# Attention ahead of a mixture of experts: where the softmax's reciprocals stand, and when its sums and scalings are issued

## The chip, the cores and the metric

The kernel runs on one core of one Trainium2 chip. The time is that of one execution on the device in microseconds; several executions give a median. Lower is better.

## The reference

Three stages follow each other; the change lies in the first, and the other two only wait for its result.

```
q_pool = q.reshape(B, H, S // 2, 2, D).mean(axis=3)      # B 4, H 8, S 1152, D 64: 576 pooled queries
scores = matmul(q_pool, k^T) / sqrt(D)                   # 576 x 1152 for each of 32 heads
attn   = exp(scores - max(scores))
attn   = attn / (sum(attn) + 1e-9)
x      = matmul(attn, v)                                 # 576 x 64 a head, together x[2304, 512]
x      = moe(x, w_gate, w1, w2)                          # 8 experts, Sinkhorn gate
out    = soft_moe(x, phi, m2_w1, m2_w2)
```

## The kernel before, in words

A phase is one head; two heads form a pair, so there are 16 pairs and 32 phases (NPH). A phase has nine slots (SLOTS), one for each 128 keys, and the main loop of `attention` goes through all slots `s` in one row: `ph` is the phase, `c` the slot in it, `u` the slot in the pair (0 to 17). What an engine does, and in which order, is written out by this loop: PE, ScalarE, VectorE and GpSimd execute what the loop emits in that order.

In each slot, `emit_E` computes the transposed scores of 128 keys against the 576 queries into one of two PSUM tiles `se` (L255), ScalarE takes the exponential into a tile `e` (L260), and GpSimd adds `e` to the running sum `acc` of the phase (L264, L266). Both inputs of that addition and its output lie in SBUF. The maxima that the exponential needs are computed a phase ahead: `emit_S` writes scores the other way round into one of two PSUM banks `S` (L226), and VectorE reduces them (L227). `first(n)` emits the next n of these, so that L226 waits for the L227 two steps before it. `emit_nm` (L230) and `emit_row` (L239, L243, L245) turn the maxima into a row that is added in the products of `emit_E`.

At the slots u = 0, 5, 9 and 14 (RUNS) there is a run: all products of `e` with v that are due (`emit_PV`, L281, into the bank `o`) are issued in one row, with two S steps ahead of them and two behind. u = 0 and 9 have c == 0, u = 5 and 14 have c == 5. A run at c == 0 finishes the phase before, and ScalarE copies `o` to the SBUF tile `oc` (L288).

The normalisation of phase ph - 1 begins at c == 5 of phase ph: `emit_sum` multiplies `acc` by ones (L296), which gives the sum over the keys on all partitions, and ScalarE writes it with 1e-9 added to the SBUF tile `rs` (L300). At c == 0 of phase ph + 1 `emit_recip` takes the reciprocals in place, in two halves of 144 columns (L304). At c == 5 of that phase `emit_O` multiplies: four operations, for each of two groups of 64 partitions one with 256 columns into the tile of x (L313) and one with 32 into the ninth tile (L314). Of the 288 columns the first 256 and the last 32 go to different tiles, `xa[2 * b + g]` and `xa[8]`.

`bank()` gives the one PSUM bank `t` (pool `ps_t`, one buffer). It is shared by the transposes of k and q (`k_bank`, `q_bank`, L163, L134), by `emit_row` and by `emit_sum`; a new user waits for the last reader of the one before. Behind the transposes of k these are ScalarE's copy (L170) and VectorE's subtraction L176, which reads `t` from PSUM and `kp` from SBUF; behind those of q, L150 and L152. The subtractions are put off by `low` and issued by `flush` behind the `emit_E` of the next slot. k's second bank is filled at u = 13, so its L176 comes just ahead of the run at u = 14; q's first one is filled at u = 3 and its L152 comes ahead of the run at u = 5.

In the last phase VectorE adds a part of the running sums itself (L272), and the loop goes on for ten slots behind it: at c == 0 phase 30 is normalised, at c == 3 the last sums are formed, at c == 6 phase 31 is normalised. From there on the matmuls of the first expert (L777 to L779 and, behind them, L796) run, with VectorE and ScalarE splitting weights and activations into high and low parts.

Of the kernel before, what the change touches and what calls it, by code (L numbers as in the profile page):

```python
# [11 lines left out]
ALU = mybir.AluOpType  # L12
# [14 lines left out]
def attention(ctx, nc, tc, q, k, v, xa, ident, ones, hooks):  # L27
# [18 lines left out]
    NPH = 2 * NPAIR  # L46
    raws = {n: {} for n in "qkv"}
    prep, M_, E_, acc_, O_, R_ = {}, {}, {}, {}, {}, {}
# [51 lines left out]
    def bank():  # L100
        return ps_t.tile([128, 512], F32, tag="t", name="t")
# [7 lines left out]
    def flush():  # L109
        while later:  # L110
            later.pop(0)()
# [66 lines left out]
    def k0(pi):  # L178
        k_bank(pi, 0, 4, half() if front[0] else bank())

    def k4(pi):
        k_bank(pi, 4, 4, half() if front[0] else bank())

    def kq8(pi):
        ps = bank()
        k_bank(pi, 8, 1, ps)
        o, st = qd[pi % 2], prep[pi]
        src = ps[:, 128:256].rearrange("p (h g x) -> p h g x", h=2, g=2)
        q1 = st["q1"][:, :, :, 256:]
        for h in range(2):  # L190
            nc.scalar.copy(o[64 * h:64 * h + 64, 64 * h:64 * h + 64], ps[64 * h:64 * h + 64, 128 + 64 * h:192 + 64 * h])
        nc.scalar.copy(q1, src)
        low(lambda: nc.vector.tensor_tensor(
            out=q1[64:128], in0=src[64:128], in1=q1[64:128].bitcast(F32), op=ALU.subtract
        ))
# [33 lines left out]
    def emit_nm(ph, x0, n):  # L229
        nc.vector.tensor_reduce(  # L230
            out=NM[ph % 2][:, x0:x0 + n, 64], in_=M_[ph][:, x0:x0 + n], axis=AX.X, op=ALU.max, negate=True
        )

    def emit_row(ph, x0, n):
        pi, h = divmod(ph, 2)
        q2 = prep[pi]["q2"][64:65]
        ps = bank()
        for x in range(n):
            nc.tensor.matmul(  # L239
                ps[:65, 128 * x:128 * x + 128], lhsT=NM[ph % 2][:, x0 + x], rhs=identr, start=True, stop=True  # L240
            )
        if x0 == 0:
            nc.scalar.copy(q2[:, :, :, 256:], ps[64:65, :128].rearrange("p (h g x) -> p h g x", h=2, g=2))  # L243
        else:
            nc.scalar.copy(q2[:, h, :, :256], ps[64:65].rearrange("p (g x) -> p g x", g=2))  # L245


    def emit_E(ph, c, between=0):
        pi, h = divmod(ph, 2)
        st, kd = prep[pi], KD[ph % 3]  # L250
        e = E_[ph, c] = e_p.tile([128, 2, 288], F32, tag="e", name="e")
        ps = ps_e.tile([128, 2, 512], F32, tag="se", name="se")[:, :, :288]
        for g in range(2):
            for z, y in enumerate((st["q1"], st["q2"])):
                nc.tensor.matmul(  # L255
                    ps[:, g], lhsT=kd[:, z, 128 * c:128 * c + 128], rhs=y[:, h, g], start=z == 0, stop=z == 1
                )
            if g == 0:
                first(between)
        nc.scalar.activation(out=e, in_=ps, func=AF.Exp, scale=1.0 / 16)  # L260

        if c == 1:
            acc_[ph] = sm_p.tile([128, 2, 288], F32, tag="acc", name="acc")
            nc.gpsimd.tensor_tensor(out=acc_[ph], in0=E_[ph, 0], in1=e, op=ALU.add)  # L264
        elif c > 1 and (ph < NPH - 1 or c < LATE):
            nc.gpsimd.tensor_tensor(out=acc_[ph], in0=acc_[ph], in1=e, op=ALU.add)  # L266
        elif c == 8:
            acc_["end"] = e
        elif c > LATE:
            if c == LATE + 1:  # L270
                acc_["late"] = sm_p.tile([128, 2, 288], F32, tag="acc", name="acc")
            nc.vector.tensor_tensor(  # L272
                out=acc_["late"], in0=E_[ph, LATE] if c == LATE + 1 else acc_["late"], in1=e, op=ALU.add
            )

    def emit_PV(ph, c):
        pi, h = divmod(ph, 2)
        if c == 0:
            O_[ph] = ps_o.tile([128, 512], F32, tag="o", name="o")
        for g in range(2):  # L280
            nc.tensor.matmul(  # L281
                O_[ph][64 * g:64 * g + 64, :288], lhsT=raws["v"][pi][:, h, c, :], rhs=E_[ph, c][:, g],
                start=c == 0, stop=c == 8,
            )
        E_.pop((ph, c))
        if c == 8 and ph < NPH - 1:
            o = sm_p.tile([128, 288], F32, tag="oc", name="oc")
            nc.scalar.copy(o, O_[ph][:, :288])  # L288
            O_[ph] = o

    def emit_sum(ph):
        ps = bank()
        ts = [acc_.pop(ph)] + ([acc_.pop("end"), acc_.pop("late")] if ph == NPH - 1 else [])
        for j, t in enumerate(ts):
            for g in range(2):
                nc.tensor.matmul(  # L296
                    ps[64 * g:64 * g + 64, :288], lhsT=ones[:, :64], rhs=t[:, g], start=j == 0, stop=t is ts[-1]
                )
        R_[ph] = sm_p.tile([128, 288], F32, tag="rs", name="rs")
        nc.scalar.activation(out=R_[ph], in_=ps[:, :288], func=AF.Identity, bias=eps)  # L300

    def emit_recip(ph, u):
        r = R_[ph][:, 144 * u:144 * u + 144]
        nc.vector.reciprocal(out=r, in_=r)  # L304

    def emit_O(ph):
        pi, h = divmod(ph, 2)
        b, hp = pairs[pi]
        o, r = O_.pop(ph), R_.pop(ph)
        for g in range(2):  # L310
            y, z = slice(64 * g, 64 * g + 64), slice(64 * h, 64 * h + 64)
            w = slice(64 * b + 32 * g, 64 * b + 32 * g + 32)
            nc.vector.tensor_tensor(out=xa[2 * b + g][z, hp, :], in0=o[y, :256], in1=r[y, :256], op=ALU.mult)  # L313
            nc.vector.tensor_tensor(out=xa[8][z, hp, w], in0=o[y, 256:288], in1=r[y, 256:], op=ALU.mult)  # L314

    firsts = [(2 * p + (x > 4), x if x < 5 else x - 4, n) for p in range(NPAIR) for x in range(9) for n in range(3)]

    def first(n=1):
        for _ in range(n):
            if firsts:  # L320
                emit_S(*firsts.pop(0))
# [31 lines left out]
    for s in range(SLOTS * NPH + 10):  # L353
        ph, c = divmod(s, SLOTS)
        pi, h = divmod(ph, 2)
        u = s % (2 * SLOTS)
        nxt, nn = pi + 1, pi + 2
        on, run = ph < NPH, u in RUNS if ph < NPH else s % 3 == 0
        for f in hooks.get(s - SLOTS * NPH, ()):
            with tc.issue_after(last_dma[0]):  # L360
                f()
        if on:
            emit_E(ph, c, int(u in BETWEEN or s in (2, 4)))
            flush()
        if run:
            if on:
                first(2)
            if 1 < ph <= NPH and c == 0:
                emit_recip(ph - 2, 0)
                emit_recip(ph - 2, 1)  # L370
            if ph > 1 and (c == 5 if on else c == 0):
                emit_O(ph - 2)
            if ph == NPH and c == 6:
                emit_recip(ph - 1, 0)
                emit_recip(ph - 1, 1)
            for g in range(max([x for x in range(s) if x % (2 * SLOTS) in RUNS], default=0), s):
                if g < SLOTS * NPH:
                    emit_PV(*divmod(g, SLOTS))
            if ph and (c == 5 if on else ph == NPH and c == 3):
                emit_sum(ph - 1)  # L380
            if on:
                first(2)
        if ph + 1 < NPH and u in (5, 14):
            emit_nm(ph + 1, 1, 4)
        if ph + 2 < NPH and u == 8:
            emit_nm(ph + 2, 0, 1)
        if ph + 1 < NPH and u in (6, 15):
            emit_row(ph + 1, 1, 4)
        if ph + 1 < NPH and u == 10:
            emit_row(ph + 1, 0, 1)  # L390
        if on and nxt < NPAIR:
            if s == 0:
                k0(nxt)
            if s == 2:
                k4(nxt)
            if u == (3 if s < SLOTS else 1):
                kq8(nxt)
            if u == (4 if s < SLOTS else 2):
                kd_dma(nxt, 0)
            if u == (4 if s < SLOTS else 3):  # L400
                q_bank(nxt, 0)
            if u == 8:
                q_bank(nxt, 1)
            if u == 9:
                q2_dma(nxt)
                kd_dma(nxt, 1)
                load_v(nxt)
        if on and nn < NPAIR:
            if u == 6:
                load_k(nn)  # L410
                load_q(nn)
            if u in (11, 13):
                pool_q(nn, u // 13)
            if u == 12:
                k0(nn)
            if u == 13:
                k4(nn)
# [1061 lines left out]
```

## Time and profile before

| | |
|---|---|
| Median of three executions | 2242.56 us (2242.03 to 2244.97) |
| The profiled execution, its own time | 2243.12 us |
| Its span in the profile | 2241.2 us |
| Attention stage | about the first 640 us of the span |
| Granted TensorE clock, mean over the span | 0.987 of full |
| Busy: PE, VectorE, ScalarE, GpSimd | 2099.8, 1497.4, 944.1, 412.6 us |

The span runs from the first to the last instruction; the execution's own time is 1.9 us longer. Busy time counts an engine's instructions from start to end; matmuls overlap in the pipeline and their ends are modelled, so PE reads as busier than it is. In a timeline the second column is a duration, `xN` means that N neighbouring records were merged, and what stands in brackets at the end is how long the engine had been idle and which instruction ended that.

### The profile page before, as it was taken

The page shows a single profiled execution, that of the slowest core. Times are in us where ns is not written, and L with a number is a line of the kernel's source. Part 1 is how long each engine was busy: PE and PEld are TensorE (multiplying, and loading weights), DVE is VectorE, ACT ScalarE, POOL GpSimd, SP SyncE. Part 2 cuts the span into 40 slices and gives each one's busy share as a digit, 9 for nine tenths or more (in the row PEclk, how much of TensorE's full clock was granted, in tenths as well). Part 3 has the DMA queues.
Part 4 walks back from the last instruction along what each step waited for, and adds up shares of the span by engine and source line. Part 5 has one row for each costly group of instructions (what it writes and reads, how often), then busy time and mean ns, then how long its engine had stood idle before and what let it go on. Part 6 is the DMA issues. An engine that isn't in the chain of part 4 may idle for free.

```text
span 2241.2 us, 40342 instructions
## 1 busy us (share of the span) xinstructions
PE 2099.8 (94%) x16382; PEld 1904.5 (85%) x16382; DVE 1497.4 (67%) x2529; ACT 944.1 (42%) x1708; POOL 412.6 (18%) x304
## 2 busy tenths in 40 slices
PE   7888888788899999999999999999999999999997
PEld 5665656565689999999999999999999999999864
DVE  5777777777785867668667757757766855544462
ACT  3444444444454445345336435435534533311232
POOL 5666666666610000000000000000000000000000
PEclk9999999999999999999999999999999999999998
DMA  7443435343332555454456445536445523487569
GB/s 176 111 96 96 111 80 119 88 106 69 86 113 114 214 191 169 168 192 159 151 198 207 160 160 184 208 127 209 168 167 178 177 74 123 151 327 264 207 218 281
DMA packets 175273, 358.41 MB, mean 160 GB/s; under 512 B 49392, under 2 KB 98096, under 8 KB 173104
## 3 DMA queue, kind: packets, MB, share of 16 engines
q1 hardware_dynamic: 172688, 354.35, 49.8%
q8 instruction: 130, 2.13, 0.4%
q10 hardware_dynamic: 2400, 1.47, 0.2%
q14 instruction: 55, 0.45, 0.1%
HBM read 274.81 MB, written 48.23 MB: 144 GB/s over the span
## 4 chain that ended last, share of the span: by engine, by line
PE 76%; DVE 16%; ACT 5%; issue 2%; DMA 1%; SPq 1%; ACTq 0%; DVEq 0%
PE y L796 28%; PE g L738 15%; PE seed L738 9%; DVE m L227 4%; PE se L255 4%; DVE x L313 3%; DVE rs L304 2%; PE S L226 2%; ACT e L260 2%; DVE x L314 2%; PE g L828 1%; PE g L829 1%; PE g L827 1%; PE y L848 1%; PE g L777 1%
## 5 line engine op out<-in xcount | busy, mean ns | idle before, releaser
L796 PE MATMUL y<-v,ho 128*128 128x256 f32 x5292 | 679.8, 284 | 3.7 <-DVE acc L808 2.6
L796 PEld LDWEIGHTS y<-v,ho 128*128 128x128 f32 x5292 | 653.8, 192 | 9.8 <-issue 4.4
L738 PE MATMUL g<-xs,w 128*128 128x256 f32 x2880 | 375.9, 283 | 0.0
L738 PEld LDWEIGHTS g<-xs,w 128*128 128x128 f32 x2880 | 359.0, 192 | 0.0
L266 POOL TENSOR_TENSOR acc<-acc,e 128x576 f32<-128x576 f32 x218 | 310.5, 1424 | 94.9 <-ACT e L260 82.7
L227 DVE TENSOR_REDUCE m<-S 128x1 f32<-128x384 f32 x432 | 226.1, 550 | 90.3 <-PE S L226 83.3
L952 POOL MEMSET HT<- 128x1024 f32 x2 | 1.9, 960 | 1484.9 <-PE g L829 1484.9
L808 DVE SCALAR_TENSOR_TENSOR acc<-y,P,acc 128x256 f32<-128x256 f32 x378 | 181.4, 480 | 117.3 <-PE y L796 114.5
L260 ACT ACTIVATE e<-se 128x576 f32<-128x576 f32 x288 | 183.7, 653 | 167.0 <-PE se L255 131.0
L712 DVE TENSOR_TENSOR ho<-hr,ho 128x512 fp32r<-128x512 f32 x189 | 130.2, 689 | 150.3 <-ACT ho L711 148.3
L738 PE MATMUL seed<-xs,w 128*128 128x256 f32 x1728 | 211.3, 283 | 0.0
L738 PEld LDWEIGHTS seed<-xs,w 128*128 128x128 f32 x1728 | 209.1, 192 | 0.0
L712 DVE TENSOR_TENSOR ho<-ht,ho 128x512 fp32r<-128x512 f32 x252 | 170.3, 686 | 50.7 <-ACT ho L711 48.5
L711 ACT CAST ho<-ht 128x512 fp32r<-128x512 f32 x252 | 150.3, 618 | 112.4 <-DVE ht L705 110.2
L255 PE MATMUL se<-q,kd 128*128 128x288 f32 x576 | 187.4, 333 | 5.6 <-ACT e L260 4.6
L226 PE MATMUL S<-kd,q 128*128 128x384 f32 x384 | 126.0, 377 | 60.0 <-DVE m L227 59.5
L255 PE MATMUL se<-qm,kd 128*128 128x288 f32 x576 | 172.5, 307 | 0.0
L281 PE MATMUL o<-e,vr 128*64 128x288 f32 x1152 | 154.4, 413 | 0.0
L226 PEld LDWEIGHTS S<-kd,q 128*128 128x128 f32 x384 | 67.9, 196 | 93.0 <-DVE m L227 56.7
L255 PEld LDWEIGHTS se<-q,kd 128*128 128x128 f32 x576 | 114.4, 199 | 17.9 <-ACT e L260 16.5
L281 PEld LDWEIGHTS o<-e,vr 128*64 128x64 f32 x1152 | 77.3, 137 | 60.9 <-issue 16.8
L705 DVE TENSOR_TENSOR ht<-hr 128x512 f32<-128x512 f32 x126 | 86.2, 684 | 54.1 <-ACT hr L747 31.8
(210 smaller groups left out, 3080.8 us busy)
## 6 DMA issues: line engine op xcount, KB each, us to landing
stg<-in_moe_w_dram SPq DMA_DIRECT2D x96, 512.0 KB, 6.0
kd<-kp SPq DMA_DIRECT2D x31, 576.0 KB, 5.7
xs<-xd0B SPq DMA_DIRECT2D x34, 512.0 KB, 4.1
xs<-xd1B SPq DMA_DIRECT2D x34, 512.0 KB, 4.1
xs<-xd2B SPq DMA_DIRECT2D x34, 512.0 KB, 4.0
xs<-xd3B SPq DMA_DIRECT2D x34, 512.0 KB, 4.3
fd<-stg SPq DMA_DIRECT2D x24, 512.0 KB, 5.7
stg<-fd SPq DMA_DIRECT2D x24, 512.0 KB, 4.5
```

What stands on the lines that cost most here:

```text
L226: nc.tensor.matmul(ps, lhsT=w, rhs=r[:, 384 * n:384 * n + 384], start=True, stop=True)
L227: nc.vector.tensor_reduce(out=M_[ph][:, x, n:n + 1], in_=ps, axis=AX.X, op=ALU.max)
L255: nc.tensor.matmul(ps[:, g], lhsT=kd[:, z, 128 * c:128 * c + 128], rhs=y[:, h, g], start=z == 0, stop=z == 1)
L260: nc.scalar.activation(out=e, in_=ps, func=AF.Exp, scale=1.0 / 16)
L266: nc.gpsimd.tensor_tensor(out=acc_[ph], in0=acc_[ph], in1=e, op=ALU.add)
L281: nc.tensor.matmul(O_[ph][64 * g:64 * g + 64, :288], lhsT=raws["v"][pi][:, h, c, :], rhs=E_[ph, c][:, g], start=c == 0, stop=c == 8,)
L705: (eng or nc.vector).tensor_tensor(out=o, in0=a, in1=b, op=op)
L711: nc.scalar.copy(o[:, 0], p)
L712: nc.vector.tensor_tensor(out=o[:, 1], in0=p, in1=o[:, 0].bitcast(F32), op=ALU.subtract)
L738: nc.tensor.matmul(o, lhsT=w[:, a, kk, cols], rhs=x[:, b, kk], start=begin, stop=kk == 1 and z == 2, skip_group_check=not first or f2 > 0,)
L796: nc.tensor.matmul(ps, lhsT=o[:, x, c], rhs=v[:, w, c], start=first and c + z == 0, stop=c + z == 5, skip_group_check=not first,)
L808: nc.vector.scalar_tensor_tensor(out=y, in0=ps, scalar=p, in1=y, op0=ALU.mult, op1=ALU.add)
```

## The change

The reciprocals no longer replace the sums in SBUF. Each half of 144 columns is written to a fresh `bank()` in PSUM, and the multiplications of that half follow at once and read it from there. The first half's part is issued at c == 0, the second half's at c == 5, both for phase ph - 2 as before. The second half has 112 columns for the tile of x and 32 for the ninth tile, so a phase now has two reciprocals and six multiplications where it had two and four. In the last phase the reciprocals stay in place. `emit_sum` is issued ahead of the products with v of its run, and ahead of the reciprocal, where it used to come behind the products.

```
--- before.py
+++ after.py
@@ -299,19 +299,21 @@
         R_[ph] = sm_p.tile([128, 288], F32, tag="rs", name="rs")
         nc.scalar.activation(out=R_[ph], in_=ps[:, :288], func=AF.Identity, bias=eps)
 
-    def emit_recip(ph, u):
-        r = R_[ph][:, 144 * u:144 * u + 144]
-        nc.vector.reciprocal(out=r, in_=r)
-
-    def emit_O(ph):
+    def emit_O(ph, u):
         pi, h = divmod(ph, 2)
         b, hp = pairs[pi]
-        o, r = O_.pop(ph), R_.pop(ph)
+        o, r, n = O_[ph], R_[ph][:, 144 * u:144 * u + 144], 144 * u
+        t = bank()[:, :144] if ph < NPH - 1 else r
+        nc.vector.reciprocal(out=t, in_=r)
         for g in range(2):
             y, z = slice(64 * g, 64 * g + 64), slice(64 * h, 64 * h + 64)
             w = slice(64 * b + 32 * g, 64 * b + 32 * g + 32)
-            nc.vector.tensor_tensor(out=xa[2 * b + g][z, hp, :], in0=o[y, :256], in1=r[y, :256], op=ALU.mult)
-            nc.vector.tensor_tensor(out=xa[8][z, hp, w], in0=o[y, 256:288], in1=r[y, 256:], op=ALU.mult)
+            m = min(n + 144, 256)
+            nc.vector.tensor_tensor(
+                out=xa[2 * b + g][z, hp, n:m], in0=o[y, n:m], in1=t[y, :m - n], op=ALU.mult
+            )
+            if u:
+                nc.vector.tensor_tensor(out=xa[8][z, hp, w], in0=o[y, 256:288], in1=t[y, 112:144], op=ALU.mult)
 
     firsts = [(2 * p + (x > 4), x if x < 5 else x - 4, n) for p in range(NPAIR) for x in range(9) for n in range(3)]
 
@@ -365,19 +367,22 @@
         if run:
             if on:
                 first(2)
-            if 1 < ph <= NPH and c == 0:
-                emit_recip(ph - 2, 0)
-                emit_recip(ph - 2, 1)
-            if ph > 1 and (c == 5 if on else c == 0):
-                emit_O(ph - 2)
-            if ph == NPH and c == 6:
-                emit_recip(ph - 1, 0)
-                emit_recip(ph - 1, 1)
+            if ph and (c == 5 if on else ph == NPH and c == 3):
+                emit_sum(ph - 1)
+            if ph > 1 and on:
+                if c == 0:
+                    emit_O(ph - 2, 0)
+                else:
+                    emit_O(ph - 2, 1)
+            elif ph == NPH and c == 0:
+                for j in range(2):
+                    emit_O(ph - 2, j)
+            elif ph == NPH and c == 6:
+                for j in range(2):
+                    emit_O(ph - 1, j)
             for g in range(max([x for x in range(s) if x % (2 * SLOTS) in RUNS], default=0), s):
                 if g < SLOTS * NPH:
                     emit_PV(*divmod(g, SLOTS))
-            if ph and (c == 5 if on else ph == NPH and c == 3):
-                emit_sum(ph - 1)
             if on:
                 first(2)
         if ph + 1 < NPH and u in (5, 14):
```

VectorE, in the first head of the second pair, from the run at c == 0 to the run at c == 5 (`m` are the maxima, `nm` their negative, `oc` the copy of the products with v, `x_80`, `x_81` and `x_88` the tiles of x). At c == 0:

```order
 L230 TENSOR_REDUCE nm_121<-m_405 128x4
 L227 TENSOR_REDUCE m_596<-S 128x1 x4
-L304 RECIPROCAL rs<-rs 128x144 x2
+L307 RECIPROCAL t<-rs 128x144
+L312 TENSOR_TENSOR x_80<-oc,t 64x144
+L312 TENSOR_TENSOR x_81<-oc,t 64x144
 L227 TENSOR_REDUCE m_596<-S 128x1 x3
```

One reciprocal has given way to two multiplications of 144 columns. At the next c == 5, on VectorE:

```order
 L152 TENSOR_TENSOR q_540<-t,q_540 64x2x256
 L227 TENSOR_REDUCE m_596<-S 128x1 x2
-L313 TENSOR_TENSOR x_80<-oc,rs 64x256
-L314 TENSOR_TENSOR x_88<-oc,rs 64x32
-L313 TENSOR_TENSOR x_81<-oc,rs 64x256
-L314 TENSOR_TENSOR x_88<-oc,rs 64x32
-L227 TENSOR_REDUCE m_762<-S 128x1 x2
+L307 RECIPROCAL t<-rs 128x144
+L312 TENSOR_TENSOR x_80<-oc,t 64x112
+L316 TENSOR_TENSOR x_88<-oc,t 64x32
+L312 TENSOR_TENSOR x_81<-oc,t 64x112
+L316 TENSOR_TENSOR x_88<-oc,t 64x32
+L227 TENSOR_REDUCE m_766<-S 128x1 x2
```

The second reciprocal stands here now, ahead of four multiplications with 112 and 32 columns in place of 256 and 32; the maxima behind them are the same (their tile has another number). On PE, at the run at c == 5 in the second head of the first pair (`S` scores for the maxima, `t` the bank, `o` the products with v):

```order
 L226 MATMUL S<-kd_125,q_303 128x384 x2
+L296 MATMUL t<-acc,ones 64x288 x2
 L281 MATMUL o<-e,vr 64x288 x10
-L296 MATMUL t<-acc,ones 64x288 x2
 L226 MATMUL S<-kd_123,q_303 128x384 x2
```

The two sums have moved ahead of the ten products with v; the pairs of S on either side stay. At the end of the stage 35 matmuls of the first expert now stand between the last products with v and the last sums, where the sums used to follow directly; ScalarE, GpSimd and the queue of SyncE have the same order as before.

## Rows read from the trace of the kernel before

**Rows 1.** Busy time of each engine in one stretch of the attention stage.

```profile
430.00:580.00 150.00, 120.95 (x796) 88.41 (x793) 113.16 (x187) 66.51 (x128) 98.41 (x70) 0.98 0.40 94
```

**Rows 2.** Chain of waits from 195 to 260 us, its shares by line.

```profile
by line: DVE m L227 16.2%; PE se L255 13.9%; DVE x L313 12.0%; DVE rs L304 11.8%; ACT e L260 8.0%; PE S L226 7.5%; DVE x L314 6.6%; DVE kp L176 4.7%; issue 4.6%; PE t L163 3.3%; DVE q L152 3.2%; ACT q L150 2.4%; ACT kp L170 1.8%; ACT qm L24
```

**Rows 3.** Groups of VectorE's instructions by form, 0 to 640 us: count, busy, mean ns.

```profile
L313 DVE TENSOR_TENSOR x<-oc,rs 64x256 f32<-64x256 f32 x62 | 69.7, 1124 | 1.4
L304 DVE RECIPROCAL rs<-rs 128x144 f32<-128x144 f32 x64 | 62.7, 1022 | 0.4
L314 DVE TENSOR_TENSOR x<-oc,rs 64x32 f32<-64x32 f32 x62 | 50.1, 808 | 0.0
...
L176 DVE TENSOR_TENSOR kp<-t,kp 128x512 fp32r<-128x512 f32 x32 | 22.0, 687 | 21.9 <-ACT kp L170 21.8
...
L176 DVE TENSOR_TENSOR kp<-t,kp 128x128 fp32r<-128x128 f32 x16 | 4.7, 291 | 17.1 <-PE S L226 16.8 <-ACT kp L170 0.3
...
L313 DVE TENSOR_TENSOR x<-o,rs 64x256 f32<-64x256 f32 x1 | 0.4, 419 | 0.1
...
L314 DVE TENSOR_TENSOR x<-o,rs 64x32 f32<-64x32 f32 x1 | 0.2, 174 | 0.0
```

**Rows 4.** Timeline, a run at c == 5 in a second head: start, duration, instruction.

```profile
242.67 0.69 DVE L176 TENSOR_TENSOR kp<-t,kp 128x512 fp32r<-128x512 f32 x1
...
243.51 0.63 PE L163 MATMUL t<-ident,kr 128*128 128x128 f32 x4 [1.17 <-DVE kp L176]
...
244.79 0.69 DVE L176 TENSOR_TENSOR kp<-t,kp 128x512 fp32r<-128x512 f32 x1 [1.43 <-ACT kp L170]
...
244.94 2.65 PE L281 MATMUL o<-e,vr 128*64 128x288 f32 x20
...
246.45 1.25 DVE L313 TENSOR_TENSOR x<-oc,rs 64x256 f32<-64x256 f32 x1
...
247.38 1.59 POOL L120 TENSOR_TENSOR qp<-qr 128x576 f32<-128x576 f32 x1
247.42 0.66 PE L296 MATMUL t<-acc,ones 128*64 128x288 f32 x4
247.62 1.40 DVE L314 TENSOR_TENSOR x<-oc,rs 64x32 f32<-64x32 f32 x1
...
248.00 0.62 PE L226 MATMUL S<-kd,q 128*128 128x384 f32 x2
248.12 0.50 ACT L300 ACTIVATE rs<-t,eps 128x288 f32<-128x288 f32 x1 [2.70 <-PE t L296]
...
248.93 1.39 POOL L266 TENSOR_TENSOR acc<-acc,e 128x576 f32<-128x576 f32 x1
...
249.03 1.58 DVE L313 TENSOR_TENSOR x<-oc,rs 64x256 f32<-64x256 f32 x1
...
250.75 1.02 DVE L227 TENSOR_REDUCE m<-S 128x1 f32<-128x384 f32 x2
...
251.36 0.44 PE L226 MATMUL S<-kd,q 128*128 128x384 f32 x1 [2.48 <-DVE m L227]
```

**Rows 5.** Timeline, a run at c == 5 in a first head.

```profile
224.47 0.69 DVE L152 TENSOR_TENSOR q<-t,q 64x512 fp32r<-64x512 f32 x1 [0.84 <-ACT q L150]
...
225.16 2.65 PE L281 MATMUL o<-e,vr 128*64 128x288 f32 x20
...
228.22 0.63 PE L226 MATMUL S<-kp,qd 128*128 128x384 f32 x2
...
229.66 1.01 DVE L227 TENSOR_REDUCE m<-S 128x1 f32<-128x384 f32 x2
```

**Rows 6.** Timeline, a run at c == 0.

```profile
235.94 1.97 DVE L304 RECIPROCAL rs<-rs 128x144 f32<-128x144 f32 x2
...
237.82 0.50 DVE L227 TENSOR_REDUCE m<-S 128x1 f32<-128x384 f32 x1
```

**Rows 7.** Busy time of each engine just behind the attention stage.

```profile
640.00:645.00 5.00, 5.00 (x44) 5.00 (x43) 4.92 (x8) 3.63 (x6) 0.00 (x0) 1.00 0.00 0
```

## The prediction

> **What bounds the kernel now.** I read four views, from wide to narrow: the busy time of the engines by stretch, the chain of waits over a few periods of the attention stage, the groups of VectorE's instructions, and the timeline around one run of each kind. In the middle of the attention stage no engine is full [rows 1]: in that row stand PE, weight loads, VectorE, ScalarE and GpSimd in this order, and VectorE has 113 of 150 us, GpSimd 98, ScalarE 67; PE's 121 is an overlapped, modelled figure. So what counts is who hands over to whom. The chain over 65 us [rows 2] goes through VectorE for more than half: the maxima (L227) 16.2%, and the normalisation, that is the reciprocals (L304) 11.8% and the products (L313, L314) 12.0% and 6.6%. The normalisation of a phase is no input of the next phase, yet it lies on the path, since the maxima that empty the two S banks stand behind it on VectorE.
>
> The second thing to see is that the products take far longer than their size. The 62 wide ones have a mean of 1.124 us, the 62 narrow ones 0.808 us; the same shapes at the very end, when GpSimd has finished, take 0.42 and 0.17 us [rows 3]. The timeline of a run at c == 5 in the second head of a pair [rows 4] shows why: the narrow product starts at 247.62, just after GpSimd started an addition (247.38, 1.59 us), and ends at 249.02, 0.05 us after it; the next wide one starts 0.10 us behind GpSimd's next addition and ends 0.29 us after that does. A product whose two inputs lie in SBUF stands still until GpSimd's instruction is over. Operations with one input in PSUM do not: L176 stays at 0.687 us for 512 elements and 0.291 for 128 [rows 3] beside a GpSimd that is busy. Behind the products, the maxima start at 250.75 and PE, which had waited 2.48 us, goes on at 251.36 [rows 4].
>
> **The change, part by part.**
>
> *Durations.* The reciprocal stays at 1.02 us for 144 columns [rows 3]; no row has one that writes to PSUM, so I bound it: nothing more, or the 0.02 us by which the fixed part of an operation on PSUM exceeds one on SBUF, below; either is small. A product with one input in PSUM is priced by L176: (687 - 291) / 384 = 1.03 ns an element and 159 ns fixed, so 0.31 us for 144 columns, 0.27 for 112, 0.19 for 32. The SBUF shapes left alone by GpSimd give (419 - 174) / 224 = 1.09 ns and 139 ns fixed. On one half of the partitions the next instruction starts some 0.08 us before the row of the one ahead ends (246.45 + 1.25 against 247.62), between the halves it does not (247.62 + 1.40 against 249.03) [rows 4]. So the four products behind the second half take 0.76 to 0.92 us, I take 0.85, and the two behind the first 0.6. Between the reciprocal and the first product, which reads its result, I leave 0.09 us, an estimate of the size of these overlaps.
>
> *The Trainium skill, Perfetto Trace Analysis, section Optimizing Scalar/DVE Operations, gives VectorE about 60 ns of data access per instruction on SBUF and about 125 ns on PSUM, a rule against this change: 65 ns more for each of the eight instructions of a phase. The fixed parts above differ by 20 ns, so the trace bears out a third of it. With the page's 65 ns the gain at c == 0 below would vanish and the sum would end at about 2211 us.*
>
> *Run at c == 5, second head* [rows 4]. The order on PE becomes S pair, sums, products with v (L281), S pair; on VectorE it becomes maxima, reciprocal, four products, maxima. The sums need the one transpose bank, which the subtraction L176 leaves at 245.48; with the 0.15 us that PE took behind the L176 before (242.67 + 0.69 to 243.51) they start at 245.63, where the products with v started at 244.94 before. This is a new wait, 0.7 us, and L281 and the S pair stand behind it on PE. Sums to Identity (L300) took 247.42 to 248.12, 0.70 us, so Identity runs from 246.33 to 246.83. The reciprocal waits for it, since it writes into the bank that Identity reads; VectorE is free at 246.45, where it began L313 before, so this second new wait is 0.4 us, and only the maxima of the next S pair are queued behind. Reciprocal to 247.85, products to 248.79. On PE the sums and L281 together take what they took, 244.94 to 248.00 = 3.06 us, so the next S pair starts at 248.69 and its first score is there 0.4 us later (as the S of 251.36 shows, 0.44), at 249.1. PE is later than VectorE here, and the maxima start at 249.1 instead of 250.75: 1.62 us gained.
>
> *Run at c == 5, first head* [rows 5]. The bank is held by L152 until 225.16; sums at 225.30, Identity to 226.5, reciprocal and products to 228.46. PE's S pair starts at 225.30 + 3.06 = 228.36, first score at 228.8. The maxima began at 229.66: 0.86 us gained. The stall of the products was shorter here to begin with.
>
> *Runs at c == 0* [rows 6]. Two reciprocals took 235.94 to 237.82, 1.88 us in steps. Now one reciprocal and two wide products, 1.02 + 0.09 + 0.6 = 1.71: 0.17 us gained. At some of these runs PE's own work may end last, so of 30 I count 25, a choice.
>
> *What follows.* The S banks, exponentials and maxima of the next slots come earlier by these amounts; they are PE, ScalarE and VectorE handing over to each other, and none is full [rows 1]. GpSimd has 98 of 150 us, and a third of the time as slack covers a pair of heads that is 2.8 us shorter. The loads of k and q are issued more than a pair ahead in the code, those of v half a pair. The order on SyncE, ScalarE and GpSimd is the same.
>
> *The end of the stage.* GpSimd has stopped, so nothing is gained there, and VectorE is full: 4.92 of 5 us in the stretch behind [rows 7]. The last head's products cost more in four pieces with a second half: for the run at c == 5, 1.02 + 0.09 + 0.85 = 1.96 against four unhindered products of 0.42, 0.17, 0.42, 0.17 less overlap, 1.1: 0.9 us lost; for the last two heads 1.71 + 1.96 = 3.67 against 3.1 each, 1.2 lost. The last sums now wait for the bank until head 30's products are through, and twelve matmul records instead of four, about 1.7 us, plus Identity's 0.5 lie between that and the last reciprocal: between 0 and 2.2 us, taken at 1.1. Together 3.2 us lost. The 35 expert matmuls that now stand ahead of the last sums keep PE busy meanwhile.
>
> *Sum.* Second heads 3 to 29: 14 x 1.62 = 22.7. First heads 2 to 30: 15 x 0.86 = 12.9. c == 0: 25 x 0.17 = 4.3. End: -3.2. Gain 36.7 us. The profiled execution took 2243.1 us, 0.6 above the median of 2242.56; 2243.1 - 36.7 = 2206.4, by the median **2206 us**.
>
> **The rivals.**
>
> *VectorE alone decides.* If the score is ready sooner than I take, the maxima start at 228.46 and 248.79, and the runs at c == 5 gain 0.3 us more: 29 x 0.3 = 9, so 2197 us; with the end costing nothing 2194. For it: PE's ends are modelled. Against it: the S pair follows twenty matmul records in order.
>
> *The sums come late.* They stand ahead of the products with v, and they need the bank and GpSimd's running sum. Each further microsecond there delays L281, the S pair and the reciprocal alike: 29 us of the gain, about 2235 us, and with 1.3 us nothing is left, 2243 us. Against it: by the code the last addition to that running sum belongs to the phase before, six slots back, and L176's and L152's ends are in the rows. For it: a wait in a long PE queue can cost more than its handover.
>
> *The products are still held.* The change then does not do what it says: an input in PSUM would not free the product from GpSimd. A held product loses 0.70 us (wide) or 0.63 (narrow) [rows 3]; six instead of four per phase would lose about 4.0 us instead of 2.7, and with 0.5 us for two more instructions and 0.4 us for the wait on Identity a phase gets 2.2 us longer: 28 x 2.2 = 62, 2305 us. Break-even lies at a mean hold of about 0.2 us. Against it: L176 has 0.687 us on average over 32, and one that was held for 0.7 us would raise that by 0.02 [rows 3]; though its PSUM operand is the first input, and here it is the second.
>
> **How the numbers follow.** A measurement of this kernel tells about 0.2%, 4.5 us, from no change. The forecast, a gain of 25 to 47 us, gets 0.70; VectorE alone, 0.12; sums late but still a gain, 0.10; nothing left of it, 0.03; products held, 0.05. So faster 0.92, same 0.03, slower 0.05. The range takes the forecast, the first rival and the better half of the second: 2186 to 2226 us.
>
> **What would show it.** Right: products of 0.19, 0.27 and 0.31 us with hardly any spread; the wait of PE's S for VectorE's maxima well below now; a reciprocal at c == 5 that waits some 0.4 us for L300; sums that start behind L176 or L152; a pair of heads shorter by about 2.8 us. Wrong: products above 0.6 us, GpSimd's additions longer than 1.42 us, or an S that now waits for the sums and gives back what VectorE saved.

## The result, and the profile after

The changed kernel takes 2205.8 us in the median (2200.4 to 2208.6, four runs), the kernel before, beside it on the same chip, 2243.8. The ratio is 0.9828, with a 95% interval of 0.9806 to 0.9849: faster by 1.7%. The forecast was 2206 us.

Each engine's busy time and its share of the chain of waits, from the page of the changed kernel:

```profile
PE 2094.6 (95%) x16382; PEld 1904.7 (86%) x16382; DVE 1435.2 (65%) x2593; ACT 943.0 (43%) x1708; POOL 408.6 (19%) x304
...
PE 82%; DVE 9%; ACT 4%; issue 2%; DMA 1%; SPq 0%; ACTq 0%; DVEq 0%
```

The chain of the kernel before:

```profile
PE 76%; DVE 16%; ACT 5%; issue 2%; DMA 1%; SPq 1%; ACTq 0%; DVEq 0%
```

VectorE's share of the chain has fallen from 16% to 9% and its busy time by 62 us; PE has 82% of the chain in place of 76%. VectorE's groups in the first 620 us (count, busy us, mean ns, idle before):

```profile
L307 DVE RECIPROCAL t<-rs 128x144 f32<-128x144 f32 x62 | 65.6, 1058 | 12.8 <-ACT rs L300 12.3
...
L312 DVE TENSOR_TENSOR x<-oc,t 64x144 f32<-64x144 f32 x62 | 18.7, 302 | 1.5
L312 DVE TENSOR_TENSOR x<-oc,t 64x112 f32<-64x112 f32 x62 | 16.7, 269 | 1.5
L316 DVE TENSOR_TENSOR x<-oc,t 64x32 f32<-64x32 f32 x62 | 11.1, 179 | 0.0
```

They answer to [rows 3]. No product is held any more: the means are those of free instructions, 0.30, 0.27 and 0.18 us, and by the view of one line the longest of all 124 wide ones takes 0.307 us. The reciprocal has a mean of 1.058 us. It now waits for Identity (ScalarE's L300), 12.3 us in all.

A run at c == 5 in a second head, the counterpart of [rows 4] (start, duration, instruction, idle time before it):

```profile
233.94 0.69 DVE L176 TENSOR_TENSOR kp<-t,kp 128x512 fp32r<-128x512 f32 x1 [1.43 <-ACT kp L170]
...
234.78 0.71 PE L296 MATMUL t<-acc,ones 128*64 128x288 f32 x4 [0.61 <-DVE kp L176]
...
235.53 0.50 ACT L300 ACTIVATE rs<-t,eps 128x288 f32<-128x288 f32 x1 [0.95 <-PE t L296]
236.06 1.06 DVE L307 RECIPROCAL t<-rs 128x144 f32<-128x144 f32 x1 [0.49 <-ACT rs L300]
236.46 1.42 POOL L120 TENSOR_TENSOR qp<-qr 128x576 f32<-128x576 f32 x1
237.15 0.26 DVE L312 TENSOR_TENSOR x<-oc,t 64x112 f32<-64x112 f32 x1
...
237.72 0.19 DVE L316 TENSOR_TENSOR x<-oc,t 64x32 f32<-64x32 f32 x1
...
238.32 1.02 DVE L227 TENSOR_REDUCE m<-S 128x1 f32<-128x384 f32 x2 [0.41 <-PE S L226]
```

The sums (L296) wait 0.61 us for the subtraction L176, which gives up the bank; the products with v (L281) follow. Identity (L300) ends at 236.03 and the reciprocal starts at 236.06, 0.49 us after VectorE had nothing else to do. GpSimd begins an addition at 236.46, and the four products run through beside it in 0.76 us. Then VectorE waits 0.41 us for PE's S pair. From the end of L176 to the first maximum it is 3.69 us; before it was 5.27 [rows 4]. In the first head it is L152's end to the first maximum:

```profile
214.18 0.69 DVE L152 TENSOR_TENSOR q<-t,q 64x512 fp32r<-64x512 f32 x1 [0.84 <-ACT q L150]
...
218.56 1.02 DVE L227 TENSOR_REDUCE m<-S 128x1 f32<-128x384 f32 x2 [0.42 <-PE S L226]
```

That is 3.69 us too, against 4.50 [rows 5]. At c == 0 one reciprocal and two products take 1.74 us from 225.12 to the maximum at 226.86, against 1.88 [rows 6]. What PE's S lost to VectorE's maxima over the stage before (us, times, longest):

```profile
PE S L226 <- DVE m L227: 76.3, 62, 2.6
```

The same wait now, and that of the reciprocal for Identity:

```profile
PE S L226 <- DVE m L227: 29.0, 62, 1.3
...
DVE t L307 <- ACT rs L300: 12.3, 29, 0.5
```

PE's sums wait for L176 at 14 second heads, 8.7 us in all.

### The profile page after: what moved, and what is told of

The parts are those of the page before. It is cut to its first block, busy times and chain, and to the rows that moved or that the text cites. A ratio compares the mean times of both kernels' runs of the same rounds, so it can differ in the third digit from the quotient of the medians.

```text
span 2203.6 us, 40450 instructions
## 1 busy us (share of the span) xinstructions
PE 2094.6 (95%) x16382; PEld 1904.7 (86%) x16382; DVE 1435.2 (65%) x2593; ACT 943.0 (43%) x1708; POOL 408.6 (19%) x304
## 4 chain that ended last, share of the span: by engine, by line
PE 82%; DVE 9%; ACT 4%; issue 2%; DMA 1%; SPq 0%; ACTq 0%; DVEq 0%
PE y L801 28%; PE g L743 15%; PE seed L743 9%; PE se L255 4%; PE o L281 4%; DVE m L227 3%; PE S L226 3%; ACT e L260 2%; PE g L833 2%; PE g L834 2%; PE g L832 2%; PE y L853 1%; DVE t L307 1%; PE y L854 1%; PE y L855 1%
## 5 line engine op out<-in xcount | busy, mean ns | idle before, releaser
L266 POOL TENSOR_TENSOR acc<-acc,e 128x576 f32<-128x576 f32 x218 | 309.1, 1418 | 62.2 <-ACT e L260 49.7
L255 PE MATMUL se<-q,kd 128*128 128x288 f32 x576 | 179.7, 321 | 9.0 <-ACT e L260 8.2
L255 PE MATMUL se<-qm,kd 128*128 128x288 f32 x576 | 165.0, 295 | 0.0
L281 PE MATMUL o<-e,vr 128*64 128x288 f32 x1152 | 153.1, 409 | 0.0
L281 PEld LDWEIGHTS o<-e,vr 128*64 128x64 f32 x1152 | 87.8, 137 | 50.5 <-issue 8.1
L255 PEld LDWEIGHTS se<-q,kd 128*128 128x128 f32 x576 | 108.9, 189 | 22.0 <-ACT e L260 20.6
```

The lines of the kernel that those rows point to most:

```text
L255: nc.tensor.matmul(ps[:, g], lhsT=kd[:, z, 128 * c:128 * c + 128], rhs=y[:, h, g], start=z == 0, stop=z == 1)
L281: nc.tensor.matmul(O_[ph][64 * g:64 * g + 64, :288], lhsT=raws["v"][pi][:, h, c, :], rhs=E_[ph, c][:, g], start=c == 0, stop=c == 8,)
```

## The experiments

Each ran beside the kernel before on the same chip; the ratio is to that. "Free" below means that a product runs at its own length.

**Reciprocals of both halves in SBUF, everything else as changed (e1).**

```
-        t = bank()[:, :144] if ph < NPH - 1 else r
+        t = sm_p.tile([128, 144], F32, tag="rt", name="rt") if ph < NPH - 1 else r
```

> The changed kernel with one thing undone: each half's reciprocals go to a fresh SBUF tile, all orders of VectorE stay. Theory 1 (a product with two SBUF inputs stands still until GpSimd's addition is over, and PSUM frees it): the six products get the holds of before, means near 0.6 to 1.1 us in place of 0.27; per pair 2.3 us at the second head's c == 5, 1.9 at the first head's, up to 1.3 at each c == 0, so 4 to 7 us a pair and 2265 to 2305 us, slower than before the change. Rival (the gain is from splitting and from the earlier sums, PSUM is incidental): 2200 to 2215 us, as the changed kernel.

2228.6 us, ratio 0.9929 (0.9912 to 0.9946): 23 us slower than the changed kernel, yet 15 us faster than before, so between the two theories. The groups of its products, and a run at c == 5 in a second head:

```profile
L312 DVE TENSOR_TENSOR x<-oc,rt 64x112 f32<-64x112 f32 x62 | 54.1, 872 | 1.5
L316 DVE TENSOR_TENSOR x<-oc,rt 64x32 f32<-64x32 f32 x62 | 26.9, 434 | 0.0
...
L312 DVE TENSOR_TENSOR x<-oc,rt 64x144 f32<-64x144 f32 x62 | 20.5, 331 | 1.5
```

```profile
209.06 1.04 DVE L307 RECIPROCAL rt<-rs 128x144 f32<-128x144 f32 x1
...
210.06 1.41 POOL L120 TENSOR_TENSOR qp<-qr 128x576 f32<-128x576 f32 x1
210.14 1.46 DVE L312 TENSOR_TENSOR x<-oc,rt 64x112 f32<-64x112 f32 x1
...
211.42 1.44 POOL L266 TENSOR_TENSOR acc<-acc,e 128x576 f32<-128x576 f32 x1
...
211.52 1.40 DVE L316 TENSOR_TENSOR x<-oc,rt 64x32 f32<-64x32 f32 x1
...
212.93 0.27 DVE L312 TENSOR_TENSOR x<-oc,rt 64x112 f32<-64x112 f32 x1
```

The hold is there, but it is not one per product. The product of 210.14 ends with the GpSimd instruction of 210.06 (211.47), the next one with that of 211.42, and then both others are free, since GpSimd has nothing more to do. In [rows 4] three products met three instructions of GpSimd. The first of these, the end of a pair of additions, those rows leave out:

```profile
244.50 2.92 POOL L266 TENSOR_TENSOR acc<-acc,e 128x576 f32<-128x576 f32 x2
```

In e1 the reciprocal, 1.04 us as ever beside GpSimd, fills this stretch, and two holds remain. At c == 0 the products of 144 columns have 331 ns, hardly a hold. So in these two runs as many products are held as GpSimd has instructions left behind the reciprocal, and moving the reciprocal there hides one.

**First half alone in SBUF (e5).**

```
-        t = bank()[:, :144] if ph < NPH - 1 else r
+        if ph == NPH - 1:
+            t = r
+        elif u == 0 and ph < NPH - 2:
+            t = sm_p.tile([128, 144], F32, tag="rt", name="rt")
+        else:
+            t = bank()[:, :144]
```

> The changed kernel with the reciprocals of the first half alone (c == 0, two wide products of 144 columns) in an SBUF tile. Theory 1: these two products are held, 0.2 to 0.65 us each as far as GpSimd is busy at c == 0; VectorE ends last there, so 30 runs lose 0.4 to 1.3 us each: 2218 to 2245 us, 2230 taken; the four products at c == 5 stay short. Rival (PSUM is incidental): 2203 to 2209 us.

2202.1 us, ratio 0.9813 (0.9799 to 0.9828): not to be told from the changed kernel. The mechanism holds and the place was wrong: in the runs at c == 0 GpSimd is through by the time the products start. The reciprocals' group, and the shortest, median and longest of the 60 products (ns):

```profile
L312 DVE RECIPROCAL rt<-rs 128x144 f32<-128x144 f32 x30 | 31.4, 1047 | 0.4
...
L317 DVE TENSOR_TENSOR x<-oc,rt x60: 301/305/1480, 67.4 to 578.2; 64x144 f32<-64x144 f32 x60
```

With a median of 305 ns the products lose nothing; their mean of 337 comes mostly from one that was held, 1480 ns in the last pair of heads. Nearly all that PSUM brings, it brings at c == 5.

**The cause taken away (e9, e10): GpSimd's additions to the running sum (L266) left out.**

```
+        elif 1 < c < 9 and ph < NPH - 1:
+            pass
         elif c > 1 and (ph < NPH - 1 or c < LATE):
```

> The kernel before with GpSimd's additions L266 left out in phases 0 to 30 (slots 2 to 8 are not added to the running sums), nothing else changed. It takes the cause of the hold away and leaves the products where they are. Theory 1: the wide products fall to about 0.42 us and the narrow ones to 0.18, with a few still held by the two pooling additions of a pair; at c == 5 PE's S pair decides, ready 2.3 us earlier than the maxima began at the second head and 1.0 at the first: 47 us gained, 2196 us (2188 to 2208). Rival (the products are long by themselves, or the gain is one of order): 2238 to 2246 us.

> The changed kernel with the same additions L266 left out in phases 0 to 30. Theory 1: its products do not meet GpSimd any more, so nothing is gained: 2202 to 2208 us, products unchanged at 0.18, 0.27 and 0.30 us. Rival (GpSimd still delays something on the path, an exponential's tile or the sums): 2180 to 2198 us.

In the kernel before, this edit gives 2184.9 us, ratio 0.9734 (0.9719 to 0.9748), 59 us faster; in the changed one it gives 2202.4, 0.9815 (0.9799 to 0.9831), no difference that can be told. The groups of the first:

```profile
L315 DVE TENSOR_TENSOR x<-oc,rs 64x256 f32<-64x256 f32 x62 | 26.0, 420 | 1.4
...
L316 DVE TENSOR_TENSOR x<-oc,rs 64x32 f32<-64x32 f32 x62 | 11.2, 181 | 0.0
...
L315 DVE TENSOR_TENSOR x<-o,rs 64x256 f32<-64x256 f32 x2 | 0.8, 424 | 0.1
```

Products with both inputs in SBUF have 420 and 181 ns once these additions are gone, where they had 1124 and 808 [rows 3], and the longest of all 62 wide ones takes 423 ns. So the hold is GpSimd's doing. That e10 gains nothing says that the 59 us of e9 are not GpSimd's load as such. The second lesson is the distance between the two: without holds the old order is 17 us faster than the new one. The change pays for its freedom; where these 17 us lie stands at the end.

**The place of the sums (e2, e3).** e2 puts them back behind the products with v in all phases but the last, in the changed kernel; e3 moves them ahead in the kernel before, and does nothing else.

```
e2:
-            if ph and (c == 5 if on else ph == NPH and c == 3):
+            if ph and (c == 5 if on else ph == NPH and c == 3) and not (ph < 31):
                 emit_sum(ph - 1)
...
                     emit_PV(*divmod(g, SLOTS))
+            if ph and (c == 5 if on else ph == NPH and c == 3) and (ph < 31):
+                emit_sum(ph - 1)
e3:
+            if ph and (c == 5 if on else ph == NPH and c == 3):
+                emit_sum(ph - 1)
...
                     emit_PV(*divmod(g, SLOTS))
-            if ph and (c == 5 if on else ph == NPH and c == 3):
-                emit_sum(ph - 1)
```

> The changed kernel with the sums put back behind the products with v, in all phases but the last. Theory 1 with PE's order as the second limit: the reciprocal no longer waits for Identity, but the sums now wait for the bank until VectorE's products are through, and the S pair behind them comes 0.43 us later at the second head and 0.6 at the first; 29 runs, 15 us: 2221 us (2213 to 2230). Rival (the gain is mostly from the earlier sums): 2235 to 2245 us. If the place of the sums does not matter: 2203 to 2209 us.

> The kernel before with one part of the change alone: the sums ahead of the products with v. Theory 1: VectorE's held products still end last at c == 5 (249.7 to 250.8 against an S pair that is ready at 249.1 in the rows of before), so 2243 us, within 5. Rival (the earlier sums carry the gain): 2210 to 2230 us. The new wait of PE for the bank, 0.7 us a run, would show as up to 10 us slower if PE were the limit.

e2: 2216.8 us, ratio 0.9880 (0.9865 to 0.9894), 11 us slower than the changed kernel. Its sums wait for the last product to leave the bank:

```profile
PE t L296 <- DVE x L316: 16.5, 29, 0.7
```

That is 0.57 us a run. e3: 2243.2 us, 0.9996 (0.9987 to 1.0005): by itself the earlier place gives nothing; the held products still end last, as was expected. It is needed only because the reciprocals now share the sums' bank; e11 below does without it.

**Without the halves (e4, e12).** Both reciprocals and four unsplit products at c == 5, in PSUM; the edit is against the kernel before, and the sums stand ahead as in the changed one.

```
     def emit_O(ph):
...
-        o, r = O_.pop(ph), R_.pop(ph)
+        o, r = O_[ph], R_[ph]
+        t = bank()[:, :288] if ph < NPH - 1 else r
+        for u in range(2):
+            nc.vector.reciprocal(out=t[:, 144 * u:144 * u + 144], in_=r[:, 144 * u:144 * u + 144])
```

> The changed kernel without the halves: both reciprocals and four unsplit products at c == 5, reciprocals in PSUM, sums ahead. Theory 1: products unhindered, but VectorE has 3.3 us behind Identity in place of 2.0, so the maxima start about 1.0 us later than PE's S pair allows at both c == 5; at c == 0 up to 0.9 us is gained in the first half of a pair's runs and little in the other; together +1 us a pair, 2221 us (2212 to 2232). If only the PSUM bank matters and the split is nothing: 2203 to 2209 us.

> The kernel e4 again, which normalised the last head twice; here once. The second time cost VectorE 3 us at the end of the stage: 2217 to 2222 us; if the end of the stage is not on the path, 2222 us as e4. Against the changed kernel's 2206 us it prices the split.

e4, whose last head is normalised twice, took 2221.9 us, 0.9901 (0.9886 to 0.9915); e12 2215.5 us, 0.9878 (0.9861 to 0.9894). The split is worth 10 us, less than the 11 to 16 expected. By the stretches between VectorE's subtractions (see "The runs" below), e12 against the changed kernel is 1.0 us longer at both runs at c == 5 and 0.95 us shorter at c == 0 ahead of a second head, as the expectation of e4 had it. The further normalisation takes 3.1 us in e4's trace; the medians differ by 6, but the two intervals overlap, so its price is not settled.

**Less waiting for the bank (e6, e7, e8).** e6 takes the last two phases' reciprocals in place; e7 issues one slot's products with v ahead of the sums (`due` lists the slots of the run); e8 does both.

```
e6:
-        t = bank()[:, :144] if ph < NPH - 1 else r
+        t = bank()[:, :144] if ph < NPH - 2 else r
e7:
...
+            if on and c == 5:
+                emit_PV(*divmod(due.pop(0), SLOTS))
             if ph and (c == 5 if on else ph == NPH and c == 3):
                 emit_sum(ph - 1)
```

> The changed kernel, but the last two phases (not only the last) take their reciprocals in place, so that the last sums need not wait for the bank. Theory: VectorE's gap of 1.1 us ahead of the last reciprocal goes and PE no longer runs ahead of VectorE by as much; 1 to 3 us gained, more if the stretch at half the clock behind it goes too: 2201 to 2205 us. Rival (nothing there is on the path): 2205 to 2207 us.

> The changed kernel with one slot's two products with v ahead of the sums at c == 5, so that PE has work while the bank is still held. Theory (PE's wait for the bank of 0.6 us is on the path, since the S pair behind the products ends last): at the second head the S pair comes up to 0.5 us earlier and VectorE, 0.15 us ahead of it now, then decides, 0.15 to 0.3 us a pair, 2 to 5 us: 2201 to 2204 us. Rival (VectorE is the limit at once, since the reciprocal comes later too): 2205 to 2212 us.

> The two edits before in one kernel. If both gain, their sum: 2198 to 2203 us; if neither, 2205 to 2208 us.

e6: 2203.2 us, 0.9820 (0.9807 to 0.9833), the direction expected but not to be told from the changed kernel; in its trace the last product starts 1.8 us earlier, counted from the L176 ahead of the first changed run (55.13 us here, 55.65 in the changed kernel). e7: 2196.5 us, 0.9789 (0.9776 to 0.9803), 9 us faster than the changed kernel where 2 to 5 had been expected: PE's wait for the bank is gone from its list, and L176 to the maximum takes 3.31 us in place of 3.69. Its profiled execution, the slowest of four, is 6 us faster, and the pairs show these; the other 3 have no row. VectorE had not 0.15 us in hand, as I had put it, but the 0.41 us of the timeline above. e8: 2195.4 us, 0.9785 (0.9771 to 0.9798), also below its range and not to be told from e7.

**A version that beats both (e11).**

```
-        t = bank()[:, :144] if ph < NPH - 1 else r
+        if u and ph < NPH - 2:
+            t = ps_e.tile([128, 2, 512], F32, tag="se", name="t")[:, 0, :144]
+        else:
+            t = r
```

with the sums behind the products with v, as before the change.

> A version built on what the runs so far show: the reciprocal of the second half goes to the free one of the two score tiles in PSUM, not to the bank of the transposes; so the sums stay behind the products with v as before, wait for no products, and the reciprocal waits for no Identity. The first half and the last two phases are taken in place in SBUF, where GpSimd is idle. Theory (products free of GpSimd, and PE's run without the wait for the bank, limit c == 5): against the changed kernel 0.66 us at the second head, about 0.2 at the first, 2 to 3 us at the end of the stage, 15 us: 2190 us (2184 to 2196). Rival (the extra user of the score tiles delays the scores of the next slots, or the order of the sums was worth something by itself): 2198 to 2215 us.

2189.5 us, ratio 0.9760 (0.9745 to 0.9774): 16 us faster than the changed kernel. Its run at c == 5 in a second head:

```profile
228.50 0.69 DVE L176 TENSOR_TENSOR kp<-t,kp 128x512 fp32r<-128x512 f32 x1 [1.43 <-ACT kp L170]
...
228.66 2.65 PE L281 MATMUL o<-e,vr 128*64 128x288 f32 x20
...
230.04 1.05 DVE L310 RECIPROCAL t<-rs 128x144 f32<-128x144 f32 x1
...
231.13 0.66 PE L296 MATMUL t<-acc,ones 128*64 128x288 f32 x4
...
231.69 0.19 DVE L319 TENSOR_TENSOR x<-oc,t 64x32 f32<-64x32 f32 x1
...
232.20 1.02 DVE L227 TENSOR_REDUCE m<-S 128x1 f32<-128x384 f32 x2 [0.32 <-PE S L226]
```

The products with v start 0.53 us before L176 ends, the reciprocal waits for nobody, the products end at 231.88, at about the same time as the sums, and the first maximum comes 3.01 us behind L176. In the run shown no scores are computed (no L255 starts on PE between 228.08 and 232.17 us), so one score tile is free; the bank of the transposes was not. e11 differs from the changed kernel in three further things, the order of the sums, the place of the first half and the end of the stage, so these 16 us are not the price of the bank alone: up to the last pair of heads the two traces differ by 13.

## Why the prediction was right, point by point

**The hold, and PSUM as the way out of it.** Shown, by e1 and e9 from two sides. One row had been misread: the products at the very end, 0.42 and 0.17 us, read their first input from PSUM, since the last phase has no copy `oc`; they are no pair of SBUF inputs left alone. e9 has such pairs, at 0.420 and 0.181 us, the same. So the 20 ns that I gave to PSUM were none, and the 65 ns an instruction between the two figures of the Trainium skill's Perfetto Trace Analysis, section Optimizing Scalar/DVE Operations, are not borne out by these products (420 and 424 ns). The reciprocal has 1.058 us into PSUM and 1.047 into a separate SBUF tile (e5), 11 ns apart.

**The runs.** Predicted gains 1.62, 0.86 and 0.17 us (second heads, first heads, c == 0); measured in the runs shown 1.58, 0.81 and 0.14. The two new waits came as put: 0.61 and 0.49 us, forecast 0.7 and 0.4. PE's S pair ends last at both c == 5. What these gains are worth on the path can be read from VectorE's subtractions, which stand ahead of the runs of every pair of heads. The kernel before, from the first pair on, and further down a pair from L176 to L152:

```profile
53.71 0.69 DVE L176 TENSOR_TENSOR kp<-t,kp 128x512 fp32r<-128x512 f32 x1 [1.43 <-ACT kp L170]
...
69.47 0.69 DVE L152 TENSOR_TENSOR q<-t,q 64x512 fp32r<-64x512 f32 x1 [0.84 <-ACT q L150]
...
79.16 0.69 DVE L152 TENSOR_TENSOR q<-t,q 64x512 fp32r<-64x512 f32 x1 [0.86 <-ACT q L150]
...
89.42 0.69 DVE L176 TENSOR_TENSOR kp<-t,kp 128x512 fp32r<-128x512 f32 x1 [1.43 <-ACT kp L170]
...
108.51 0.69 DVE L152 TENSOR_TENSOR q<-t,q 64x512 fp32r<-64x512 f32 x1 [0.84 <-ACT q L150]
...
206.39 0.69 DVE L176 TENSOR_TENSOR kp<-t,kp 128x512 fp32r<-128x512 f32 x1 [1.43 <-ACT kp L170]
...
224.47 0.69 DVE L152 TENSOR_TENSOR q<-t,q 64x512 fp32r<-64x512 f32 x1 [0.84 <-ACT q L150]
```

The changed kernel, from the same instruction on:

```profile
55.65 0.69 DVE L176 TENSOR_TENSOR kp<-t,kp 128x512 fp32r<-128x512 f32 x1 [1.43 <-ACT kp L170]
...
72.02 0.69 DVE L152 TENSOR_TENSOR q<-t,q 64x512 fp32r<-64x512 f32 x1 [0.84 <-ACT q L150]
...
80.91 0.69 DVE L152 TENSOR_TENSOR q<-t,q 64x512 fp32r<-64x512 f32 x1 [0.87 <-ACT q L150]
...
91.23 0.69 DVE L176 TENSOR_TENSOR kp<-t,kp 128x512 fp32r<-128x512 f32 x1 [1.43 <-ACT kp L170]
...
107.58 0.69 DVE L152 TENSOR_TENSOR q<-t,q 64x512 fp32r<-64x512 f32 x1 [0.84 <-ACT q L150]
```

| Stretch | The run in it | Before, us | After, us |
|---|---|---|---|
| 1: L152 to the next L152 | c == 5, first head | 9.69 | 8.89 |
| 2: that L152 to L176 | c == 0 ahead of a second head | 10.26 | 10.32 |
| 3: that L176 to the next L152 | c == 5, second head, and c == 0 behind it | 19.09 here, 18.08 further down | 16.35 |
| 3 in the first pair | the same, without products at c == 5 | 15.76 | 16.37 |

All other pairs repeat these numbers; their medians are 9.71 and 8.89 in stretch 1, 10.27 and 10.29 in stretch 2. Stretch 3 of the kernel before has two lengths, 18.1 in four of thirteen pairs and 19.0 in nine (why, below); in the changed kernel it is 16.36. A pair of heads is thus 0.8 us shorter at the first head, 1.7 at the second, and nothing at the c == 0 between them: 2.5 us, where 2.8 had been forecast. So half of the runs at c == 0 gain nothing, although VectorE's own part there is 0.14 us shorter, and the first pair, which has the earlier sums but no products yet, loses 0.6 us that were not in the forecast. Over the stage the runs give about 35 us in place of 39.9.

**The end of the stage.** Forecast: 3.2 us lost. From the last phase's second addition on VectorE (L272, at 629.83 before and 587.81 after) to the end of the normalisation (640.61 and 601.53) it is 10.8 us before and 13.7 after: 2.9 lost. The gap ahead of the last head's reciprocal, taken at 1.1 us in the forecast, in the changed kernel:

```profile
597.88 1.05 DVE L307 RECIPROCAL rs<-rs 128x144 f32<-128x144 f32 x1 [1.14 <-ACT rs L300]
```

**What the forecast did not have.** The two traces do not start alike. At the L176 at the head of the two lists, ahead of any instruction that was changed, the changed kernel is 1.9 us late (55.65 against 53.71 us). By the starts of L272 the stage had gained 42.0 us, so 44.0 counted from that L176: 9 us more than the runs give. The granted clock is the likely rest. In ten of the fourteen stretches behind a second head's run, TensorE was at 0.5 of full, its lower level of 1.2 GHz, for some 3.5 us, and in the changed kernel nowhere in the stage. One of these stretches of the kernel before, behind the run of 89.42 us, and an undisturbed one, behind that of 206.39 (busy time of PE, weight loads, VectorE, ScalarE, GpSimd, then the granted clock):

```profile
96.00:99.00 3.00, 2.94 (x13) 2.93 (x14) 1.59 (x4) 1.23 (x2) 0.89 (x1) 0.50 0.23 91
213.00:216.00 3.00, 2.60 (x17) 2.17 (x18) 1.91 (x5) 2.13 (x4) 1.38 (x1) 1.00 0.22 87
```

Then two of the changed one, in the stage and behind it:

```profile
75.00:575.00 500.00, 432.77 (x2895) 321.06 (x2890) 343.98 (x731) 242.36 (x459) 354.94 (x253) 1.00 0.44 103
616.00:620.00 4.00, 4.00 (x21) 4.00 (x21) 3.97 (x8) 3.06 (x6) 0.00 (x0) 0.50 0.00 0
```

What ran ahead of nine of the falls was PE's wait of about 2.5 us for the held products [rows 4]; the tenth, at 598 us, came behind one of 1.65 us. Four waits of 2.4 to 2.6 us had no fall behind them. That is what gives stretch 3 its two lengths: the nine pairs with a fall have 19.0 us there, the four without 18.1, so a fall costs 0.9 us, and ten of them 9 us (an estimate, with the tenth counted like the others). This closes the sum; but no experiment held the clock apart from the holds. Against that, 1.5 us of the gain were lost again behind the stage: 39.1 us at the end of the normalisation, 37.6 in the span. There, from 615 to 621 us, the changed kernel's PE is at the lower clock, after two waits of 0.9 us close together; the profile of e5 has no such stretch, so it need not come in each execution. The mechanism of the forecast and its large terms, the runs at c == 5 and the end of the stage, were therefore right, but that the sum came so close is partly luck: its terms measured some 32 us in place of 36.7, the falls of the clock added 9, and the late start and the stretch behind the stage took 3.4.

**The rivals.** VectorE alone was not the limit: it waits 0.4 us for PE at both runs. The sums did not come late. That held products would make it slower was mis-sized: I counted one hold per product, and a mean hold of 0.2 us as the point of no gain; in e1 the four products at c == 5 have 0.6 and 0.25 us of hold, 0.3 in the mean of all six, and the kernel is still 15 us faster than before. Some 10 of these are its shorter pairs (0.7 us each at full clock); its trace also has fewer falls of the clock in stretch 3, four against nine.

## What to carry to other kernels

Where a two-input operation of VectorE takes several times its length, lay the timeline of GpSimd beside it: if it ends with GpSimd's instruction, one input in PSUM may free it as it did here, and the place is worth choosing, since a bank that others wait for gives part of the gain back (here up to 13 us of 54, the order of the sums included). In the runs shown here the holds go by the other engine's instructions and not by one's own, so an instruction that is not held, put in that stretch, hides one. And look where the released engine goes next: here 0.4 us of VectorE's time at each run was already idle behind PE.

## What was not expected of the hardware

TensorE's clock, above: behind the second heads' runs ten falls to the lower level in the kernel before, nine of them behind a wait of 2.5 us; in the changed kernel none there, and one behind the stage, behind two waits of 0.9 us. e9, e10 and e11 have 1.00 over the 500 us from 75 to 575, the kernel before and e3 0.97; a single fall does not show in such a mean, and e10 has one, at 199 to 202 us, behind waits of 1.2 and 0.6 us that the changed kernel has at every second head without a fall. Not all long waits lead to one either (213 us has none), and what decides it stays open.

The 17 us between e9 and e10 have their rows. By the stretches above e10's pairs are 16.35, 8.78 and 10.29 us where e9's are 15.74, 8.74 and 10.25: 0.7 us a pair, some 10 us over the stage. The earlier sums cost 0.6 us in the first pair, the end of the stage 2.9, and two falls of the clock in e10's profiled execution, the one above and one in the first pair, 1.7 us each.
